# A spectral filter and a gated feed-forward on one core: loads reordered and tables joined at the start of the kernel

## The chip, the cores and the metric

The kernel runs on one core of a Trainium2 chip. The metric is the device time of one execution, in microseconds (us); lower is better. The time before is 865.39 us, the median of 3 runs (865.05 to 866.06).

## The reference

Each of 8 sequences of 3008 rows with 256 channels is filtered in the frequency domain, and every row of the result goes through a normalised, gated feed-forward layer:

```python
X = np.fft.rfft(x, axis=1)                       # x: 8 x 3008 x 256, float32
F = (filt_r + 1j * filt_i)[None, :, :]           # 1505 x 256 each
y = np.fft.irfft(X * F, n=x.shape[1], axis=1)
rows = y.reshape(24064, 256)
xn = rows / sqrt(mean(rows * rows) + 1e-6) * rms_g
g = xn @ w_gate                                  # 256 x 1536
out = (silu(g) * (xn @ w_val)) @ w_out           # 1536 x 256
```

## The kernel before

A transform of length 3008 = 47 x 64 is done in two steps of matrix products, with tables in place of sines. For one sequence b the stages are: the 64-point step of x with the table wa (`a0_unit` for the first sequence, `a_unit` for the others), a turn of the axes, the 47-point step with the middle table wb (`b_unit`), the product with the filter (`s_part`, on the vector engine, DVE, with the filter held transposed in the tile ff), the way back with the tables wi (`bi_unit`) and wai (`n_unit`), and the norm. The feed-forward then runs over items (b, m, jt): 8 sequences, 6 blocks of rows, 12 slices of the 1536 columns. `gv` makes the two first products of an item on the tensor engine (PE), `down` the third.

From the second sequence on, the transform's units are slipped between the items by a planner with costs per engine. The change lies ahead of that: in the part written out by hand for the first sequence, where nothing of the feed-forward can run yet. The whole order is manual; each engine executes its instructions in the order in which they are written.

The loads are issued from two queues, those of SP and of POOL (GpSimd). POOL also computes, and its DMA issues stand in its instruction order; each of its transfers waits until the one issued eight places earlier has landed. In order POOL issues: the four chunks of the first x (`x_load`, L188; float32 in memory, cast to float16, 384 KB each as written), five of six filter calls (`f_load`, L384, 512 KB each: three blocks of rows, imaginary and real part), the middle table wb in two halves (L632), the back table wi (L633), weights (`w_load`, L596), then the filter's negated copies (`f_neg`, L411, and `f_last`, L407), the last weights and the output weights (`wo_load`, L600), the four chunks of the second x (L697), and twelve operations that multiply the weights by the norm's gain (`w_gain`, L608). SP issues the identity idf, the first filter call, the tables wa, ident and wai, and three very short rows, the tails (last row of the filter, gain), all in the first 4 us.

PE works through: five fills (`fill`, a matrix product on zeros whose result is not used, L428), two `f_unit`s (L391: four transposes of a filter block, which ACT, the scalar engine, copies into ff), fills, the six groups of `a0` (L359) with fills and the transposes of the tails (L659, L660) between them, two `f_unit`s, then eight `tr0_unit`s (L369, the turn of the axes; DVE copies each out) alternating with six more `f_unit`s, one more `f_unit`, and then the loop over p. There `b_unit` (L243, tile psb) makes the product with wb, `s_part` on DVE (L233, L236) multiplies by the filter, `yt0_unit` (L420, psy) and `bi_unit` (L287, psi) go on. The list `od` gives the order of the sixteen units; a unit 2g + dh covers four steps of the middle transform, k = 4g to 4g + 3, for the half dh of the channels, and its s_part needs ff for these k and this half: the real part for e = 0, the imaginary part and its negative (from `f_neg`) for e = 1. Every f_unit writes into all k of one half.

After the loop, SP issues four transposing loads (`t4_load`, L301, t<-uu), one for each six rows. The first block of rows takes a way of its own (`t4_first`, `first_norm`), and the second (`n_first`, L485) waits for the first two of these loads and stands on PE behind the third item. From there on PE has items to do without a break.

Of the kernel before, what the change touches and what calls it, by code (L numbers as in the profile page):

```python
# [10 lines left out]
FP32 = mybir.dt.float32  # L11
FP16 = mybir.dt.float16
# [8 lines left out]
P = 128  # L21
# [5 lines left out]
K2 = 32  # L27
# [4 lines left out]
S_INV_A = 0.25  # L32
Y_SCALE = N * S_INV_B * S_INV_A
XC = 6
NXC = H // XC
# [3 lines left out]
def _make_tables():  # L39
    n2 = np.arange(N2)  # L40
    wa = np.zeros((P, P))
    wai = np.zeros((P, P))
    for h in range(2):
        r = slice(h, P, 2)
        for k2 in range(K2):
            c = np.cos(2 * np.pi * ((n2 * k2) % N2) / N2)
            s = np.sin(2 * np.pi * ((n2 * k2) % N2) / N2)
            re = 4 * k2 + 2 * h
            wa[r, re] = c
            wai[re, r] = c * (1.0 if k2 == 0 else 2.0)  # L50
            if k2 == 0:
                alt = 1.0 - 2.0 * (n2 % 2)
                wa[r, re + 1] = alt
                wai[re + 1, r] = alt
            else:
                wa[r, re + 1] = -s
                wai[re + 1, r] = -2.0 * s
    n1 = np.arange(N1)
    rows = (n1 // H) * 2 * H + n1 % H
    re, im = rows, rows + H  # L60
    wb = np.zeros((P, K2, KR))
    wi0 = np.zeros((KR, KR))
    for k2 in range(K2):
        for q in range(SL):
            if q < H:
                k = k2 + 64 * q
                sign = 1.0
            else:
                j = q - H + 1
                k = 64 * j - (k2 if k2 else 32)  # L70
                sign = -1.0
                if j == H and k2:
                    continue
            th = 2 * np.pi * ((n1 * k) % N) / N
            c, sn = np.cos(th), np.sin(th)
            if k == 0 or k == NF - 1:
                sn = np.zeros(N1)
            if k2:
                wb[re, k2, q] = c
                wb[im, k2, q] = sign * sn  # L80
                wb[re, k2, SL + q] = -sn
                wb[im, k2, SL + q] = sign * c
            else:
                part = re if q < H else im
                wb[part, k2, q] = c
                wb[part, k2, SL + q] = -sn
                m = 1.0 if k in (0, NF - 1) else 2.0
                wi0[q, part] = m * c
                wi0[SL + q, part] = -m * sn
    f = np.float16  # L90
    r = np.arange(KR)
    wi = np.zeros((P, K2, KR))
    wi[:KR] = wb[:KR].transpose(2, 1, 0)
    wi[:KR, 0, :] = wi0
    wi[:, :, (r % H) * NR + r // H] = wi * S_INV_B
    return (wa.astype(f), (wai * S_INV_A).astype(f), wb.astype(f), wi.astype(f), np.eye(P).astype(f),
            np.eye(P).astype(np.float32))


@with_exitstack  # L100
def kernel(
# [10 lines left out]
):  # L112
    nc = tc.nc

    wa_np, wai_np, wb_np, wi_np, id_np, if_np = _make_tables()
    wa_d = nc.inline_tensor(wa_np, name="wa_t").ap()
    wai_d = nc.inline_tensor(wai_np, name="wai_t").ap()
    wb_d = nc.inline_tensor(wb_np, name="wb_t").ap()
    wi_d = nc.inline_tensor(wi_np, name="wi_t").ap()
    id_d = nc.inline_tensor(id_np, name="id_t").ap()  # L120
    if_d = nc.inline_tensor(if_np, name="if_t").ap()

    z_d = nc.dram_tensor("z_tmp", (B, K2, KR, D), FP16, kind="Internal").ap()

    glob = ctx.enter_context(tc.tile_pool(name="glob", bufs=1))
# [16 lines left out]
    psM = ctx.enter_context(tc.tile_pool(name="psM", bufs=1, space=bass.MemoryType.PSUM))  # L142
    psB = ctx.enter_context(tc.tile_pool(name="psB", bufs=1, space=bass.MemoryType.PSUM))

    wa = glob.tile([P, P], FP16)
    wai = glob.tile([P, P], FP16)
    ident = glob.tile([P, P], FP16)
    idf = glob.tile([P, P], FP32)
    wb = glob.tile([P, K2, KR], FP16)
    wi = glob.tile([P, K2, KR], FP16)  # L150
    uu = glob.tile([P, H, 2, P], FP16)
# [17 lines left out]
    def raw(src, row, ap):  # L169
        return bass.AP(tensor=src.tensor, offset=src.offset + row * D, ap=ap)  # L170
# [204 lines left out]
    fst = {}  # L375
    FR4 = 4

    def f_load(i, f, eng):
        if i not in fst:
            fst[i] = stg.tile([P, 2, FR4, D], FP32, tag="stg", name="fs")  # L380
        t = fst[i]
        row = FR4 * P * i if i < 2 else NF - 1 - FR4 * P
        for src in ((filt_i, filt_r)[f],):
            eng.dma_start(t[:, f].rearrange("p a d -> p (a d)"),  # L384
                                raw(src, row, [[FR4 * D, P], [1, FR4 * D]]))

    def f_unit(i, f, dh, e):
        t = fst[i]
        ps = bank(1 + "AV".index(e), "psf").rearrange("p (a q) -> p a q", a=FR4)
        for a in range(FR4):  # L390
            nc.tensor.transpose(ps[:, a, :], t[:, f, a, ds(dh * P, P)], idf)  # L391
        v = ps.rearrange("p a (q s) -> p s a q", s=16)
        fk = ff[:, dh, 0:K2].rearrange("p (t k) c -> p t k c", k=4)
        fu = ff[:, dh, 1:K2 + 1].rearrange("p (t k) c -> p t k c", k=4)[:, ::-1, ::-1, :]
        lo = SL * (1 + f) + 8 * i
        hi = lo + H
        if i < 2:
            copy(e, fk[:, :, :, lo:lo + 8], v[:, 0:8])
            copy(e, fu[:, :, :, hi:hi + 8], v[:, 8:16])
        else:  # L400
            copy(e, fk[:, :, :, lo:lo + 8], v[:, 8:16])
            copy(e, fu[:, :, :, hi:hi + 7], v[:, 0:8, :, 1:8])

    def f_last():
        v = ff.rearrange("p e k (s q) -> p e k s q", s=3)
        for dh in range(2):
            nc.gpsimd.tensor_copy(out=v[:, dh, 0, 1:3, H:SL - 1], in_=v[:, dh, K2, 1:3, H:SL - 1])  # L407

    def f_neg(k0, n, dhs=(0, 1)):
        for dh in dhs:  # L410
            nc.gpsimd.tensor_scalar(out=ff[:, dh, k0:k0 + n, 0:SL], in0=ff[:, dh, k0:k0 + n, SL:2 * SL],  # L411
                                    scalar1=-1.0, scalar2=1.0, op0=ALU.mult, op1=ALU.mult)
# [12 lines left out]
    def fill(n, bk=0):  # L425
        ps = bank(bk, "pf")
        for _ in range(n):
            nc.tensor.matmul(ps, ss3[0][:, 0, 0, :], ss3[0].rearrange("p k e q -> p (k e q)")[:, 0:512], start=True, stop=True)  # L428
# [183 lines left out]
    with tc.manual_schedule():  # L612
# [2 lines left out]
        nc.scalar.activation(out=warm, in_=epsb.to_broadcast([P, 4]), func=AXT.Sqrt)  # L615
        for c in range(NXC):
            x_load(0, c)
        nc.sync.dma_start(idf, if_d)
        f_load(0, 0, nc.sync)
        nc.sync.dma_start(wa, wa_d)  # L620
        nc.sync.dma_start(ident, id_d)
        nc.sync.dma_start(wai, wai_d)
        tail = op.tile([P, 4, D], FP32, tag="o3", name="tail")
        for f, src in ((0, filt_i), (1, filt_r)):
            nc.sync.dma_start(tail[0:1, f, :], raw(src, NF - 1, [[D, 1], [1, D]]))
        nc.sync.dma_start(tail[0:2, 2, 0:P], moe_rms_g.rearrange("(a p) -> a p", p=P))
        f_load(0, 1, nc.gpsimd)
        for i in range(1, 3):
            for f in range(2):
                f_load(i, f, nc.gpsimd)  # L630
        for h in range(2):
            nc.gpsimd.dma_start(wb[:, ts(h, K2 // 2), :], wb_d[:, ts(h, K2 // 2), :])  # L632
        nc.gpsimd.dma_start(wi, wi_d)  # L633
        w_load(0)
        w_load(1)
# [10 lines left out]
                for dh in range(2):  # L646
                    a0_unit(gq, dh, E[dh], 1 + dh)

        fill(5)
        for dh in range(2):  # L650
            f_unit(0, 0, dh, "A")
        fill(2)
        a0(0)
        fill(3)
        a0(1, 2)
# [7 lines left out]
        copy("V", gsb, psg[:, 4:6])  # L663
        fill(2)
        a0(3)
        fill(4)
        a0(4, 5)
        for dh in range(2):
            f_unit(0, 1, dh, "A")
        todo = {g: (1, *divmod(g, 2)) for g in range(4)}  # L670
        todo[4], todo[6] = (2, 0, 0), (2, 1, 0)
        for g in range(8):
            tr0_unit(g, "V")
            if g in todo:
                f_unit(*todo[g], "A")
        f_unit(2, 0, 1, "A")
        f_neg(4, 4, (0,))
        f_neg(8, 8, (0,))
        f_neg(4, 4, (1,))
        f_neg(8, 8, (1,))  # L680
        UN = K2 // 2
        od = [2, 4, 3, 5, 6, 7, 0, 1] + list(range(8, UN))
        for p in range(UN + 3):
            if p < UN:
                b_unit(0, od[p], (0, 3)[p % 2])
                s_part(0, od[p], 1)
            if p == 0:
                f_unit(2, 1, 1, "A")
                f_last()
                f_neg(0, 4)  # L690
                w_load(2)
                wo_load(0)
                f_neg(16, 16)
                wo_load(1)
                wo_load(2)
                for c in range(NXC):
                    x_load(1, c)  # L697
                for q in range(3):
                    w_gain(q)
            if p < 2:  # L700
                fill(2, 2)
            if 2 <= p < UN + 1:
                yt0_unit(od[p - 2], "A", 1)
            if p == UN + 1:
                yt0_unit(UN - 1, "V", 1, slice(0, 2))
                yt0_unit(UN - 1, "A", 0, slice(2, 4))
            if 4 <= p < UN + 3:
                bi_unit(0, od[p - 4], "AV"[p == UN + 1], 2)
            if UN + 1 <= p < UN + 3:
                fill(1, 1)  # L710
# [100 lines left out]
        for b in range(1, B):  # L811
            t = (b - 1) * 72
# [73 lines left out]
```

## Time and profile before

| | |
|---|---|
| median of 3 runs | 865.39 us (865.05 to 866.06) |
| the profiled execution's own time | 865.26 us |
| its span, first to last instruction | 863.5 us |
| granted clock of PE, mean | 0.999 |
| busy share of the span: PE, ACT, DVE, POOL | 99%, 71%, 64%, 34% |
| packets on the queues of SP (q1) and POOL (q0) | 190040 and 8352 |

The span runs from the first to the last instruction; some time lies around it. A line of the timeline gives the start in us, the length in us, the engine, the line of the kernel, the operation, the tiles (written <- read), and in brackets how long the engine stood idle before it and what ended that. A line of the transfers gives the tiles, the queue, the operation, the count, the size of one, and the time in us from issue to landing. PE is busy nearly all the time by the page, but fills count as busy, and so do waits inside a group.

In the first 50 us, PE is busy (us, of 5 us each):

```
from     0-10  10-15  15-20  20-25  25-30  30-35  35-40  40-45  45-50
PE       7.21   4.06   5.00   4.94   4.87   5.00   4.67   4.62   4.26
DVE      2.60   3.06   3.36   4.75   5.00   5.00   3.79   2.68   2.14
```

(The first column covers 10 us.) The DMA engines write 198 to 222 GB/s while x is loaded (they read it in float32, twice as many bytes), and 406 to 422 GB/s in the filter calls.

### The profile page before, as it was taken

Reading aid. Unit: us, or ns where it says so; the run is one execution under the profiler, and the core shown is the slowest. Engines: PE = TensorE matmul, PEld = TensorE weight load, DVE = VectorE, ACT = ScalarE, POOL = GpSimd, SP = SyncE. Lnnn points to the kernel's source line nnn. Section 1 sums busy time; section 2 is a strip of 40 time slices with the busy share of each in tenths; the row PEclk is TensorE's granted clock in tenths of the full one; section 3 lists DMA queues with packets and bytes.
Section 4 is the critical chain, followed back from the end, with each engine's and each line's share of the span. In section 5 each row is a group of like instructions: output and inputs, shape, how many; then the busy total and the mean of one; then the engine's idle time right before and its main releaser. Section 6 shows DMA issues by size and latency. Waiting matters only on the chain.

```text
span 863.5 us, 17023 instructions
## 1 busy us (share of the span) xinstructions
PE 852.5 (99%) x6142; PEld 533.2 (62%) x6142; DVE 556.9 (64%) x925; ACT 613.7 (71%) x1340; POOL 296.8 (34%) x344
## 2 busy tenths in 40 slices
PE   8999999999999999999999999999999999999997
PEld 6755666566665666666666666666666666665664
DVE  4857655776666666666666676667666666555554
ACT  5887787777578756887578866888567765777443
POOL 5814841453144321534034430444123430132000
PEclk9999999999999999999999999999999999999999
DMA  9996688775975566646655658433564331521101
GB/s 283 279 179 138 135 168 167 129 137 124 196 146 120 132 150 110 148 110 143 136 127 115 130 103 173 115 87 95 136 127 93 94 72 42 125 53 49 62 25 50
DMA packets 198621, 107.98 MB, mean 125 GB/s; under 512 B 158982, under 2 KB 182920, under 8 KB 198536
## 3 DMA queue, kind: packets, MB, share of 16 engines
q1 hardware_dynamic: 190040, 86.04, 44.4%
q0 software_dynamic: 8352, 20.71, 12.4%
q8 instruction: 48, 0.79, 0.4%
q14 instruction: 37, 0.30, 0.1%
q10 hardware_dynamic: 144, 0.13, 0.0%
HBM read 45.78 MB, written 35.65 MB: 94 GB/s over the span
## 4 chain that ended last, share of the span: by engine, by line
PE 95%; DMA 2%; DVE 1%; ACT 1%; SPq 0%; issue 0%
PE po L565 28%; PE pg L548 28%; PE pv L548 28%; PE psb L243 3%; PE psi L287 2%; PE psn L316 2%; PE psa L208 2%; DMA tail<-in_moe_rms_g_dram 1%; DMA t<-uu 1%; PE psy L420 1%; PE psf L391 0%; PE pst L369 0%; DVE s L233 0%; DVE s L236 0%; DVE hh L553 0%
## 5 line engine op out<-in xcount | busy, mean ns | idle before, releaser
L553 DVE TENSOR_TENSOR hh<-pv,sg 128x512 f16<-128x512 f32 (+2 forms) x578 | 391.7, 678 | 287.3 <-ACT sg L552 222.2
L552 ACT ACTIVATE sg<-pg 128x512 f16<-128x512 f32 (+2 forms) x578 | 337.8, 585 | 216.7 <-PE pg L548 212.4
L548 PE MATMUL pg<-xn,wg 128*128 128x512 f16 (+2 forms) x1156 | 337.9, 374 | 0.0
L548 PE MATMUL pv<-xn,wv 128*128 128x512 f16 (+2 forms) x1156 | 337.8, 374 | 0.0
L565 PE MATMUL po<-wo,hh 128*128 128x256 f16 x2256 | 332.6, 272 | 0.0
L565 PEld LDWEIGHTS <-hh 128*128 128x128 f16 x2256 | 213.5, 98 | 105.3 <-issue 0.6
L270 POOL TENSOR_TENSOR ss<-s,s 128x384 f16<-128x384 f16 x112 | 102.0, 911 | 273.0 <-DVE s L236 245.3
L548 PEld LDWEIGHTS <-wv 128*128 128x128 f16 x1156 | 113.0, 98 | 130.6
L548 PEld LDWEIGHTS <-wg 128*128 128x128 f16 x1156 | 111.5, 98 | 16.9 <-issue 0.2
L342 POOL TENSOR_TENSOR xt<-y,rho 128x1024 f16<-128x1024 f32 (+1 forms) x46 | 85.4, 1857 | 2.9
L324 ACT ACTIVATE junk<-y 128x256 f16<-128x256 f32 x180 | 74.3, 413 | 2.8
L233 DVE TENSOR_TENSOR s<-psb,ff 128x384 f16<-128x384 f32 x124 | 67.8, 547 | 0.0
L236 DVE TENSOR_TENSOR s<-psb,ff 128x384 f16<-128x384 f32 x124 | 67.8, 547 | 0.0
L197 ACT ACTIVATE uu<-psi 128x384 f16<-128x384 f32 (+1 forms) x127 | 61.7, 486 | 1.5 <-PE psb L243 0.5
L197 ACT ACTIVATE y<-psn 128x512 f32<-128x512 f32 (+1 forms) x95 | 55.8, 588 | 4.2
L287 PEld LDWEIGHTS <-yt 96*128 96x128 f16 x512 | 35.4, 97 | 26.7 <-issue 1.0
L334 POOL TENSOR_TENSOR rho<-u,mhalf 128x4 f32<-128x4 f32 (+1 forms) x46 | 46.5, 1010 | 3.8
L332 POOL TENSOR_SCALAR u<-ss 128x4 f32<-128x4 f32 (+1 forms) x46 | 8.9, 194 | 104.3 <-ACT junk L324 103.3
L197 ACT ACTIVATE t<-psa 128x512 f16<-128x512 f32 x71 | 42.0, 595 | 3.2 <-PE psa L208 1.7
L287 PE MATMUL psi<-wi,yt 96*128 96x96 f16 x512 | 42.9, 205 | 0.1
L243 PE MATMUL psb<-wb,t 96*128 96x96 f16 x480 | 40.2, 206 | 0.5 <-DVE s L236 0.3
L243 PEld LDWEIGHTS <-t 96*128 96x128 f16 x480 | 28.7, 97 | 13.8 <-DVE s L236 3.9
(98 smaller groups left out, 366.1 us busy)
## 6 DMA issues: line engine op xcount, KB each, us to landing
out_dram<-o SPq DMA_DIRECT2D x40, 512.0 KB, 3.6
xc<-in_x_dram POOLq DMA_DIRECT2D x31, 384.0 KB, 6.0
z_tmp<-t SPq DMA_DIRECT2D x28, 384.0 KB, 2.6
t<-z_tmp SPq DMA_DIRECT2D x28, 384.0 KB, 6.1
out_dram<-o SPq DMA_DIRECT2D x7, 384.0 KB, 2.7
fs<-in_filt_r_dram POOLq DMA_DIRECT2D x3, 512.0 KB, 12.1
ws<-in_moe_w_gate_dram POOLq DMA_DIRECT2D x3, 512.0 KB, 11.5
ws<-in_moe_w_val_dram POOLq DMA_DIRECT2D x3, 512.0 KB, 11.7
```

The source lines that it names most:

```text
L197: nc.scalar.activation(out=out, in_=in_, func=AXT.Copy, **({} if scale is None else {"scale": scale}))
L233: eng.tensor_tensor(out=o, in0=ps, in1=f1, op=ALU.mult)
L236: eng.tensor_tensor(out=o, in0=ps[:, :, ::-1, :], in1=f2, op=ALU.mult)
L243: nc.tensor.matmul(ps[:, ts(k, KR)], st[b]["t2"][kk // KC][:, kk % KC, ds(dh * P, P)], wb[0:KR, kk, :], start=True, stop=True)
L270: nc.gpsimd.tensor_tensor(out=ss3[g % 3][:, :, dh, 0:KR], in0=s[0], in1=s[1], op=ALU.add)
L287: nc.tensor.matmul(ps[:, k, :], yt[0:KR, k, dh, :], wi[0:KR, 4 * g + k, :], start=True, stop=True)
L324: nc.scalar.activation(out=junk, in_=y[:, i, ts(u, D)], func=AXT.Square, accum_out=ss[:, 2 * i + u:2 * i + u + 1])
L342: nc.gpsimd.tensor_tensor(out=xt[:, 0:n, :], in0=y.rearrange("p a (u d) -> p (a u) d", u=2)[:, 0:n, :], in1=rho[:, 0:n].unsqueeze(2).to_br ...
L548: nc.tensor.matmul(ps[:, 0:w], wt[:, dt_, ts(jt, P)], xn[:, q0:q1, dt_, :], start=(dt_ == 0), stop=(dt_ == 1))
L552: nc.scalar.activation(out=sg[:, c], in_=pg[:, 0:w], func=AXT.Silu)
L553: nc.vector.tensor_tensor(out=hh[:, c], in0=pv[:, 0:w], in1=sg[:, c], op=ALU.mult)
L565: nc.tensor.matmul(po[s4 // 2][:, s4 % 2, :], hh[:, ts(s4, P)], wo[:, jt, :], start=(jt == 0 and s4 % 2 == 0), stop=(jt == JT - 1 and (s4 ...
```

## The change

- Four small arrays become one: wa, wai, ident and the float32 identity are one array of 128 x 640 float16 (`tab`), loaded by one DMA on SP; the tiles are views of it. Ahead of the tails, SP now issues one load where it issued five.
- All six filter calls are issued by POOL, behind the first x.
- The middle table is loaded as 8 and 24 of its 32 steps in place of two halves of 16, and the 8 go ahead of the sixth filter call.
- On PE the two f_units that stood ahead of the first a0 go behind the last; ten fills in place of five and two stand at the start, and three in place of four ahead of the last a0. The eight f_units of the first two blocks and one of the third alternate with the tr0_units; one more of the third precedes the loop over p, and two follow the first b_unit.
- `od` begins 2, 3, 4 in place of 2, 4, 3; the negated copies are made in another order, three of the four early ones behind the first b_unit.
- On POOL the third and fourth chunk of the second x are issued behind the twelve gain operations.

```diff
+    tab = np.concatenate([wa.astype(f), (wai * S_INV_A).astype(f), np.eye(P).astype(f),
+                          np.eye(P).astype(np.float32).view(f)], axis=1)
+    return tab, wb.astype(f), wi.astype(f)
...
+    tab = glob.tile([P, 5 * P], FP16)
+    wa, wai, ident = (tab[:, ts(i, P)] for i in range(3))
+    idf = tab[:, 3 * P:5 * P].bitcast(FP32)
...
-        nc.sync.dma_start(idf, if_d)
-        f_load(0, 0, nc.sync)
-        nc.sync.dma_start(wa, wa_d)
-        nc.sync.dma_start(ident, id_d)
-        nc.sync.dma_start(wai, wai_d)
+        nc.sync.dma_start(tab, tab_d)
...
-        f_load(0, 1, nc.gpsimd)
-        for i in range(1, 3):
-            for f in range(2):
-                f_load(i, f, nc.gpsimd)
-        for h in range(2):
-            nc.gpsimd.dma_start(wb[:, ts(h, K2 // 2), :], wb_d[:, ts(h, K2 // 2), :])
+        for n in range(6):
+            if n == 5:
+                nc.gpsimd.dma_start(wb[:, 0:8, :], wb_d[:, 0:8, :])
+            f_load(*divmod(n, 2))
+        nc.gpsimd.dma_start(wb[:, 8:K2, :], wb_d[:, 8:K2, :])
...
-        fill(5)
-        for dh in range(2):
-            f_unit(0, 0, dh, "A")
-        fill(2)
+        fill(10)
         a0(0)
...
-        fill(4)
+        fill(3)
         a0(4, 5)
-        for dh in range(2):
-            f_unit(0, 1, dh, "A")
-        todo = {g: (1, *divmod(g, 2)) for g in range(4)}
-        todo[4], todo[6] = (2, 0, 0), (2, 1, 0)
+        todo = [(i, f, dh) for i in range(2) for f in range(2) for dh in range(2)]
+        for u in todo[0:2]:
+            f_unit(*u, "A")
+        todo = {g: u for g, u in enumerate(todo[2:] + [(2, 0, 0)])}
         for g in range(8):
             tr0_unit(g, "V")
             if g in todo:
                 f_unit(*todo[g], "A")
-        f_unit(2, 0, 1, "A")
+        f_unit(2, 1, 0, "A")
         f_neg(4, 4, (0,))
-        f_neg(8, 8, (0,))
-        f_neg(4, 4, (1,))
-        f_neg(8, 8, (1,))
         UN = K2 // 2
-        od = [2, 4, 3, 5, 6, 7, 0, 1] + list(range(8, UN))
+        od = [2, 3, 4, 5, 6, 7, 0, 1] + list(range(8, UN))
...
             if p == 0:
+                f_unit(2, 0, 1, "A")
                 f_unit(2, 1, 1, "A")
+                f_neg(4, 4, (1,))
+                f_neg(8, 8)
...
-                for c in range(NXC):
+                for c in range(2):
                     x_load(1, c)
                 for q in range(3):
                     w_gain(q)
+                for c in range(2, 4):
+                    x_load(1, c)
```

More of the change, by code (lines that the diff above doesn't have):

```diff
@@ L95, in _make_tables @@
     wi[:, :, (r % H) * NR + r // H] = wi * S_INV_B
-    return (wa.astype(f), (wai * S_INV_A).astype(f), wb.astype(f), wi.astype(f), np.eye(P).astype(f),
-            np.eye(P).astype(np.float32))
+    tab = np.concatenate([wa.astype(f), (wai * S_INV_A).astype(f), np.eye(P).astype(f),
+                          np.eye(P).astype(np.float32).view(f)], axis=1)
+    return tab, wb.astype(f), wi.astype(f)
 @with_exitstack
@@ L113 @@
     nc = tc.nc
-    wa_np, wai_np, wb_np, wi_np, id_np, if_np = _make_tables()
-    wa_d = nc.inline_tensor(wa_np, name="wa_t").ap()
-    wai_d = nc.inline_tensor(wai_np, name="wai_t").ap()
+    tab_np, wb_np, wi_np = _make_tables()
+    tab_d = nc.inline_tensor(tab_np, name="tab_t").ap()
     wb_d = nc.inline_tensor(wb_np, name="wb_t").ap()
     wi_d = nc.inline_tensor(wi_np, name="wi_t").ap()
-    id_d = nc.inline_tensor(id_np, name="id_t").ap()
-    if_d = nc.inline_tensor(if_np, name="if_t").ap()
     z_d = nc.dram_tensor("z_tmp", (B, K2, KR, D), FP16, kind="Internal").ap()
@@ L143 @@
     psB = ctx.enter_context(tc.tile_pool(name="psB", bufs=1, space=bass.MemoryType.PSUM))
[L145 to L148, printed above, removed]
+    tab = glob.tile([P, 5 * P], FP16)
+    wa, wai, ident = (tab[:, ts(i, P)] for i in range(3))
+    idf = tab[:, 3 * P:5 * P].bitcast(FP32)
     wb = glob.tile([P, K2, KR], FP16)
@@ L376, with f_load @@
     FR4 = 4
-    def f_load(i, f, eng):
+    def f_load(i, f):
         if i not in fst:
@@ L383, in f_load @@
         for src in ((filt_i, filt_r)[f],):
-            eng.dma_start(t[:, f].rearrange("p a d -> p (a d)"),
+            nc.gpsimd.dma_start(t[:, f].rearrange("p a d -> p (a d)"),
                                 raw(src, row, [[FR4 * D, P], [1, FR4 * D]]))
```

## The prediction

> **What bounds the kernel now.** I read the page first (PE busy 99% of the span of 863.5 us, 95% of the chain that ended last), then that chain in order of time, then the timeline and the landing of single transfers in the first 60 us, the only stretch in which the changed lines run. Of the chain (start, length, what):
>
> ```profile
> 3.75 7.59 DMA tail<-in_moe_rms_g_dram
> ...
> 14.43 1.07 PE psf L391 x8
> ...
> 21.84 0.62 DVE t2o L199
> 22.51 0.56 DVE s L233
> ...
> 42.16 6.04 DMA t<-uu
> 48.24 0.40 PE psn L485 x4
> ```
>
> The reader sees three limits in turn: arrivals up to 14.4 us, PE and DVE up to 42, then a transposing transfer of L301 that holds PE at 48.24. From there PE is full. What the change is worth is therefore read from one number: when the second L485 group can start. The timeline has PE's part of it:
>
> ```profile
> 13.28 1.06 PE L359 MATMUL psa<-wa,xc 128*128 128x128 f16 x16
> 14.43 1.07 PE L391 MATMUL psf<-idf,fs 128*128 128x128 f32 x8
> ...
> 47.11 0.40 PE L485 MATMUL psn<-wai,t 128*128 128x128 f16 x4
> 48.24 0.40 PE L485 MATMUL psn<-wai,t 128*128 128x128 f16 x4 [0.74 <-DMA t<-uu]
> ```
>
> The first L485 group starts where the work before it ends; the second finds PE idle for 0.74 us. So an earlier start can win 0.74 us and whatever the first 47 us shrink by, but only if that transfer also lands earlier; each us that it lands later is lost one for one.
>
> **The start of the kernel.** The x loads (L188) are issued by POOL from 1.25 us. The fourth is issued at 3.11 and lands 9.9 us later, at 13.0; the third lands near 11.1, so one x load takes 1.9 us of the DMA engines. SP's first filter call comes in ahead of x. What x would do alone, an x load issued at 53.38 with nothing ahead of it shows (first line; 53.38 to 58.1); one issued at 226.40 took 5.4 (second line):
>
> ```profile
> xc<-in_x_dram POOLq DMA_DIRECT2D x1, 384.0 KB, 4.7
> ...
> xc<-in_x_dram POOLq DMA_DIRECT2D x1, 384.0 KB, 5.4
> ```
>
> Nothing in the trace shows an x load first in an empty queue, so I bound it by these two and take 4.7, as only one small table load precedes it: x lands at 5.95, 7.85, 9.75 and 11.65 (upper bound 12.35), against 13.0. The filter calls behind it took 1.3 us each before (landing at 14.3, 15.55, 16.85, 18.1, 19.4): now 12.95, 14.25, 15.55, 16.8, 18.1, then 0.5 for a quarter of the middle table (two halves of 384 KB took near 1.0 each), and the sixth call at 19.9, 0.5 later than the last one before.
>
> The single table array costs nothing: SP has four issues of 0.36 to 0.45 us fewer ahead of the tail loads, which landed at up to 11.38 and held PE for 0.85 us. That wait goes, but its gain is inside the x gain, since the next a0 group needs the third x anyway. Two more fills (18 for 16, 0.21 to 0.43 each) run while PE waits for x; without that cover they would cost 0.4 to 0.9.
>
> **The filter calls on PE.** Before, the first filter group after a0 starts at 14.43, 1.4 after the last x landed. Now 11.65 + 1.4 = 13.05, and its data are there at 12.95. But more work now lies behind it. Between 14.43 and the first psb at 22.08 stood 8 tr0 units and 9 f_units at 0.445 each (17 x 0.445 = 7.6); now 8 and 10: the first psb at 13.05 + 18 x 0.445 + 0.1 = 21.15, a gain of 0.93. The second b_unit is now the odd half of the group (od begins 2, 3 instead of 2, 4), so it needs the very last f_unit: that one starts near 21.9, ends 22.5, and ACT needs 0.66 for each of the last two, to 23.4. DVE then starts the second unit at 23.45, against 23.51. After it DVE runs without a gap in both (0.93 per unit). So of the 1.4 us that x arrives earlier, next to nothing (0.06) reaches the loop of b_units: 0.9 goes to two f_units that used to fill the wait for x, the rest to ACT's pair.
>
> One row makes it worse. Instructions come in by DMA too (48 packets on q8 in the page, one for each 250 or so of PE's instructions). The packet records show the first, of 16 KB at 19.39 that took 1.08 us, and from then on one DMA engine ends about 1.6 us behind the others: the middle table's first half landed 2.55 after the last filter call, for 0.95 of data. The same place in PE's program comes near 18.6 now, and then it is the sixth filter call that is late: 21.5 for 19.9, with PE ready for it at 20.7. That would put the b_units 0.75 later than before. I give it six in ten; the bounds of this part are thus -0.6 (x landing as early as the data allow) and +0.8.
>
> **The second x and POOL.** POOL before:
>
> ```profile
> 30.13 2.47 POOL L188 DMA_DIRECT2D xc<-in_x_dram  x4
> 32.36 1.64 POOL L608 TENSOR_SCALAR wg<-ws,gsb 128x512 f16<-128x512 f32 x2
> ...
> 40.35 0.41 POOL L296 COPY left<-uu 128x128 f16<-128x128 f16 x1
> ```
>
> Two x issues (0.62 each) move from 31.4 to behind the twelve gain operations, which then end 1.25 earlier. Ahead of them f_neg now waits once for ACT and has 0.42 more to do in that place: +0.3, or +1.05 with the late filter call. So the two x loads are issued near 39.4 (40.15) and 40.0 (40.8). Behind them on POOL stand only the copy of L296 and the rho of L505, 11.6 us later: no price there. Their users, the a_units of the third and fourth chunk, run after 55: none either.
>
> The price is on the DMA engines. SP issues the transposing loads at 39.57. Before, x queued until 44.1 (its last chunk, issued at 31.97, took 12.1), the first chunk of t landed at 47.06 and the second at 48.2. Now the last x ends, by the 4.7 row, at 39.4 + 4.7 + 1.9 = 46.0 or, with the late filter call, at 46.75; by the 5.4 row at 47.45 at most: 1.9 to 3.35 later than before. I take 46.4, between the first two. Whether a transposing load waits for x that was issued about the same time, another place shows. Behind the x load of 226.40, a store and a transposing load landed like this, and without x (issued at 223.09) like the third line:
>
> ```profile
> out_dram<-o SPq DMA_DIRECT2D x1, 512.0 KB, 6.3
> t<-uu SPq DMA_TRANSPOSE x1, 7.1
> ...
> t<-uu SPq DMA_TRANSPOSE x1, 4.9
> ```
>
> The packet records agree: from 227.5 to 230.7 x packets alone. So SP's transfers stand behind x. Before, the second chunk landed 4.1 after x ended; 1.1 of that was a stop from 45.5 to 46.7 at an instruction packet. Without the stop: 46.4 + 3.0 = 49.4, which is 1.2 later than 48.2. With it 50.5 and more; if the transposing load comes first (-2), 47.3.
>
> [...]
>
> **Sum.** b_units 0 to +0.75, hidden under the wait at 48; wait of L485 for t: +1.2. 863.5 + 1.2 = 864.7 of span; the same execution took 865.26 and the median of three is 865.39, 0.13 away. Prediction 866.5.
>
> **The rivals.**
> - *Slower beyond doubt*: the late filter call and the instruction packet both hit. The x loads go out at 40.15, end at 47, and the stop of 1.1 still follows: chunk two at 47 + 4.1 = 51.1, +2.9, 868.2. For it: both packets come at a place of PE's program, not at a time. Against: the second one may pass while t waits anyway. It decides once x ends after 46.8.
> - *No change*: the transposing loads are paced by SP's issue (2.5 to 3.2 us each before) and by that stop, not by x. Then 48.2 stays: 865.3. Against: single loads of this kind took 4.4 to 4.9, not 7.5.
> - *Faster*: t's first chunk enters before x (39.57 against 39.4 to 40.15 is close) and passes. PE then never waits: -0.74, and with x landing early another -0.6 to -1.1: 864.5 to 863.5, middle 864.1.
> - *That part of it does nothing*: if the first x still starts only at 4.0, as its packets did before, x lands about 0.6 later than I say; the sum at 48 stays.
>
> **Chances.** Forecast (865.8 to 867.2 is its own range) 0.40; slower rival 0.22; no change 0.14; faster rival 0.24. About 0.2% or 1.7 us is what a measurement here tells from no change. Slower by more: the slower rival and a third of the forecast, 0.35. Faster by more: half of the faster rival, 0.13. Within: 0.52. Range 864.0 to 868.3, which leaves out the ends of both outer rivals.
>
> **What would show it.** Right: first L359 near 6, last x landing near 11.7, the f_unit after a0 near 13.05, first psb between 21.1 and 22, DVE's second unit no earlier than 23.4, the second L485 near 49.4 with over 1.5 us idle before it. Wrong: if the second L485 starts before 48, the collision did not happen; if psb starts before 20.5, I have overrated the f_units; if the time differs by what nothing before 50 us shows, the whole reading fails.

## The result and the profile after

The changed kernel takes 870.40 us (median of 6 runs, 869.30 to 871.53) beside 865.22 us (median of 6, 864.76 to 866.06) of the kernel before: ratio 1.006, 95% interval 1.0047 to 1.0073. It is slower by about 5.2 us. The profiled execution took 870.39 us, its span is 868.6 us, 5.1 more than before, and the mean granted clock of PE is 0.998.

Line numbers from here on are those of the changed kernel where it is read: the 47-point product psb is L240 (L243 before), s_part L230 and L233 (L233, L236), a filter unit L388 (L391), the back product psn of the norm block L482 (L485), the transposing load L298 (L301). The chain of work that ended last, in order of time (start, length, what), shows where the limits lie now:

```profile
2.59 7.05 DMA xc<-in_x_dram
9.93 11.20 DMA fs<-in_filt_r_dram
...
23.98 0.56 DVE s L230
...
41.80 10.40 DMA t<-uu
52.25 0.61 PE psn L482 x4
```

New are the x load at its head, where a tail load stood, and the last filter call, up to 21.1; the transposing transfer takes 10.40 where it took 6.04. The units between them stand as they did. The timeline of PE has the same from the engine's side (start, length, operation, idle time before it and what ended that):

```profile
5.96 0.62 PE L356 MATMUL psa<-tab,xc 128*128 128x128 f16 x8 [0.81 <-DMA xc<-in_x_dram]
...
11.54 0.96 PE L356 MATMUL psa<-tab,xc 128*128 128x128 f16 x14 [0.47 <-DMA xc<-in_x_dram]
12.93 1.06 PE L388 MATMUL psf<-tab,fs 128*128 128x128 f32 x8 [0.43 <-DMA fs<-in_filt_i_dram]
...
21.27 0.63 PE L388 MATMUL psf<-tab,fs 128*128 128x128 f32 x4 [0.53 <-DMA fs<-in_filt_r_dram]
21.73 0.34 PE L240 MATMUL psb<-wb,t 96*128 96x96 f16 x4
...
47.07 0.59 PE L545 MATMUL pv<-xn,wv 128*128 128x512 f16 x2
50.88 0.40 PE L482 MATMUL psn<-tab,t 128*128 128x128 f16 x4 [3.22 <-DMA t<-uu]
52.25 0.61 PE L482 MATMUL psn<-tab,t 128*128 128x128 f16 x4 [0.97 <-DMA t<-uu]
52.65 1.06 PE L562 MATMUL po<-wo,hh 128*128 128x256 f16 x4
```

Up to 13 us the start is 1.5 us ahead of before (the first filter group after a0 stood at 14.43), at the first psb 0.35 ahead (21.73 for 22.08), and DVE's second unit is 0.47 late (23.98 for 23.51). PE's last ready product ends at 47.66 (50.88 less 3.22), 0.55 later than the first psn group started before; then PE waits 3.22 and 0.97 us, where it waited 0.74. The last line tells of a second loss: four products of 128x256 take 1.06 us there; the same group took 0.60 before, as its line there shows:

```profile
48.48 0.60 PE L565 MATMUL po<-wo,hh 128*128 128x256 f16 x4
```

The table by stretches says why (stretch, us, then busy time of PE, PEld, DVE, ACT and POOL, and last the granted clock, the DMA share and GB/s):

```profile
48.00:50.00 2.00, 0.00 (x0) 0.00 (x0) 0.65 (x1) 0.00 (x0) 0.00 (x0) 1.00 1.13 89
...
52.00:54.00 2.00, 1.75 (x10) 1.24 (x11) 0.00 (x0) 1.10 (x3) 0.00 (x0) 0.51 1.12 215
54.00:56.00 2.00, 2.00 (x10) 0.96 (x9) 0.47 (x1) 1.07 (x2) 0.00 (x0) 0.64 0.51 94
```

From 48 to 50 PE does nothing, and the DMA engines are busy but move 89 GB/s. From 52 on the granted clock is half (0.50 from 52.1 to 55.4): 0.51 and 0.64 as means of two stretches of 2 us make 1.96 and 1.44 us at half clock, 3.4 us in all. Behind 60 us no wait of PE differs from before. The transfers that were in flight at that time (tiles, queue, operation, size, us from issue to landing):

```profile
xc<-in_x_dram POOLq DMA_DIRECT2D x1, 384.0 KB, 5.2
xc<-in_x_dram POOLq DMA_DIRECT2D x1, 384.0 KB, 9.7
...
t<-uu SPq DMA_TRANSPOSE x1, 10.8
t<-uu SPq DMA_TRANSPOSE x1, 10.4
```

The two moved x loads landed at 45.23 and 50.24, the two chunks of t at 50.84 and 52.20 (47.06 and 48.20 before). So the second chunk is 4.0 us late, and PE's second psn group with it (52.25 for 48.24). The two transposing loads were issued about when they were before (at 40.05 and 41.80, for 39.57 and 42.16), so it is their transfer that is late, not their start. Behind the second psn group PE loses 1.55 us more, at the lower clock: its last group of products starts 5.56 us later than before (timeline of the changed kernel, then of the kernel before).

```profile
862.43 1.47 PE L562 MATMUL po<-wo,hh 128*128 128x256 f16 x12
```

```profile
856.87 1.47 PE L565 MATMUL po<-wo,hh 128*128 128x256 f16 x12
```

The span grows by 5.1 and not by 5.56, because in the profiled execution of the kernel before the time from the end of that group to the end of the span is 0.4 us longer.

### The profile page after: what moved, and what is told of

The parts are those of the page before. It is cut to its first block, busy times and chain, and to the rows that moved or that the text cites. A ratio compares the mean times of both kernels' runs of the same rounds, so it can differ in the third digit from the quotient of the medians.

```text
span 868.6 us, 17024 instructions
## 1 busy us (share of the span) xinstructions
PE 854.0 (98%) x6144; PEld 532.8 (61%) x6144; DVE 557.0 (64%) x925; ACT 613.8 (71%) x1340; POOL 297.5 (34%) x345
## 4 chain that ended last, share of the span: by engine, by line
PE 94%; DMA 3%; DVE 1%; ACT 1%; issue 0%; POOL 0%; SPq 0%; POOLq 0%
PE po L562 28%; PE pg L545 28%; PE pv L545 28%; PE psb L240 3%; PE psi L284 2%; PE psn L313 2%; PE psa L205 2%; DMA fs<-in_filt_r_dram 1%; DMA t<-uu 1%; DMA xc<-in_x_dram 1%; PE psy L417 1%; DVE s L233 0%; DVE hh L550 0%; DVE s L230 0%; ACT sg L549 0%
## 5 line engine op out<-in xcount | busy, mean ns | idle before, releaser
L230 DVE TENSOR_TENSOR s<-psb,ff 128x384 f16<-128x384 f32 x124 | 67.8, 547 | 1.5 <-ACT ff L194 1.5
L233 DVE TENSOR_TENSOR s<-psb,ff 128x384 f16<-128x384 f32 x124 | 67.8, 547 | 0.0
L331 POOL TENSOR_TENSOR rho<-u,mhalf 128x4 f32<-128x4 f32 (+1 forms) x46 | 46.5, 1011 | 3.8
L240 PE MATMUL psb<-wb,t 96*128 96x96 f16 x480 | 40.2, 206 | 0.5 <-DVE s L233 0.3
L240 PEld LDWEIGHTS <-t 96*128 96x128 f16 x480 | 28.7, 97 | 13.9 <-DVE s L233 3.8
```

Of the source, the lines that this page charges most:

```text
L230: eng.tensor_tensor(out=o, in0=ps, in1=f1, op=ALU.mult)
L233: eng.tensor_tensor(out=o, in0=ps[:, :, ::-1, :], in1=f2, op=ALU.mult)
L240: nc.tensor.matmul(ps[:, ts(k, KR)], st[b]["t2"][kk // KC][:, kk % KC, ds(dh * P, P)], wb[0:KR, kk, :], start=True, stop=True)
```

## The experiments

The theory after this reading: (1) the two x loads behind the gain operations meet the transposing loads on the DMA engines, and each holds the other up; (2) PE's long wait then lowers its clock; (3) the new order at the start gives next to nothing. Rivals: the new start itself is slower; the single table array or the new order of units costs time; the x loads are an innocent bystander of an instruction packet of 16 KB. In each block of experiments the kernel before was run again on the same chip: 865.50 us (median of 21) in the first, 865.67 us (median of 33) in the second, 865.55 us (one run) in the third.

**All x loads back ahead of the gain operations, the rest of the change kept (e1_x_back).**

```diff
-                for c in range(2):
+                for c in range(NXC):
                     x_load(1, c)
                 for q in range(3):
                     w_gain(q)
-                for c in range(2, 4):
-                    x_load(1, c)
```

> The changed kernel with all four chunks of the second x issued ahead of the gain operations again; the new start stays. Theory (the two late x loads hold the transposing loads of t): the second chunk of t lands between 47.5 and 49.5, as before the change, the second L482 group starts there, PE's clock stays at 1.0, and the time is 865.0 to 866.3. Rival (the new start with its late sixth filter call costs the time): 869 or more, with t landing late all the same.

Measured 865.61 us (865.01 to 865.90, 11 runs), ratio 1.0001 (0.9992 to 1.001). The last x landed at 44.40, the chunks of t at 47.38 and 48.54. The timeline of PE has the wait of before again, and quick products behind it (0.60, as before, at a granted clock of 1.00):

```profile
48.58 0.40 PE L482 MATMUL psn<-tab,t 128*128 128x128 f16 x4 [0.76 <-DMA t<-uu]
48.82 0.60 PE L562 MATMUL po<-wo,hh 128*128 128x256 f16 x4
```

So the whole loss hangs on the place of these two loads, and all other parts of the change together are worth nothing in time, within 0.1%, as long as PE waits for t.

**Only this part, in the kernel before (e2_x_alone).**

```diff
-                for c in range(NXC):
+                for c in range(2):
                     x_load(1, c)
                 for q in range(3):
                     w_gain(q)
+                for c in range(2, 4):
+                    x_load(1, c)
```

> The kernel before with nothing but the third and fourth chunk of the second x moved behind the gain operations. Theory (x behind the gain operations holds t): t's second chunk lands at 50.5 to 52.5, PE waits 3 to 5 us at L485, 868.5 to 871. Rival (only both parts together are slow, because the new start is 0.5 late): below 867.

Measured 871.47 us (870.05 to 873.01, 4 runs), ratio 1.0069 (1.0055 to 1.0083): the part alone does all of the damage, a little more than in the changed kernel and than was expected (up to 871). The profiled execution is the slowest of the four, with a longer wait of PE than in the changed kernel and the low clock behind it for twice as long: the granted clock is 0.87, 0.50, 0.50, 0.50 and 0.93 in the stretches of 2 us from 50 to 60, which makes 6.8 us at half clock (timeline, L485 in this file):

```profile
52.46 0.61 PE L485 MATMUL psn<-wai,t 128*128 128x128 f16 x4 [4.36 <-DMA t<-uu]
53.82 0.61 PE L485 MATMUL psn<-wai,t 128*128 128x128 f16 x4 [0.75 <-DMA t<-uu]
54.23 1.06 PE L565 MATMUL po<-wo,hh 128*128 128x256 f16 x4
```

**The changed kernel with sixteen fills in PE's wait (e3_warm).** They do not shorten the wait; they only keep PE busy in it.

```diff
+        at(2, fill, 16)
         at(2, n_first, 1)
```

> The changed kernel with 16 more fills on PE ahead of the first group that waits for t (about 3.5 us of unused products in a stretch in which PE stands idle for 3.2). Nothing arrives earlier. Theory (the granted clock falls to 0.5 after the idle stretch and PE runs at half speed from 52.3 to 55.4, which costs 1.1 to 1.3 of the 5.1): clock 1.0 throughout, 869.0 to 869.5. Rival (all of the loss is the wait): 870.2 or more.

Measured 868.56 us (868.23 to 868.88, 4 runs), ratio 1.0035 (1.0021 to 1.0049): 1.84 us less than the changed kernel, more than expected. The timeline:

```profile
47.44 3.62 PE L425 MATMUL pf<-ss 128*128 128x512 f16 x16
51.12 0.38 PE L482 MATMUL psn<-tab,t 128*128 128x128 f16 x4
52.10 0.40 PE L482 MATMUL psn<-tab,t 128*128 128x128 f16 x4 [0.60 <-DMA t<-uu]
52.33 0.60 PE L562 MATMUL po<-wo,hh 128*128 128x256 f16 x4
```

The second psn group starts 0.15 earlier than without the fills (52.10 for 52.25), and the products behind it are quick again (0.60 for 1.06); the granted clock is 1.00 from 48 to 54. Between the two spans lie 1.6 us (868.6 to 867.0; 3.4 us at half clock would lose 1.7). Of the 5.6 us by which PE's last products are late in the changed kernel, some 1.6 thus belong to the clock and 4.0 to the wait itself.

**As e1, with two fills in place of ten at the start (e4_few_fills).** It asks whether the first 16 KB instruction packet, at 18.47, comes at a count of PE's instructions.

```diff
-        fill(10)
+        fill(2)
         a0(0)
```

> As e1_x_back, with two fills in place of ten at the start (eight products less ahead of everything, 16 PE instructions). Theory (a 16 KB instruction packet comes at a place of PE's program and makes one DMA engine late, and the sixth filter call with it): the packet comes near 19.3 in place of 18.5, the sixth call lands at 19.8 to 20.3 in place of 21.1, and the first psb starts up to 0.9 earlier; the time is the same as e1 or up to 0.8 less. Rival (the engine is late at a time of its own, or the call is late for another reason): it lands at 21.1 again.

Measured 865.35 us (865.09 to 866.04, 11 runs), ratio 1.0000 (0.9991 to 1.0009). The packet came at 18.45 with some 26 of PE's recorded instructions fewer ahead of it, and the sixth filter call landed at 21.09 as before. The idea of a count fell; what sets the packet's time is open. That a late DMA engine and this packet belong together stays an association: no run moved the one without the other. For the time it does not matter, since e4 and e1 agree.

**The fourth x load after the wait, the other three ahead of the gain operations (e5_x3_far), and the same one move in the kernel before (e6_before_x3_far).** If the collision is the cause, one load fewer in the queue at 40 us must also end the 0.74 us that PE waited before the change.

```diff
-                for c in range(2):
+                for c in range(3):
                     x_load(1, c)
                 for q in range(3):
                     w_gain(q)
-                for c in range(2, 4):
-                    x_load(1, c)
...
         at(4, q_unit, 1)
+        at(5, x_load, 1, 3)
```

> The changed kernel with three chunks of the second x ahead of the gain operations and the fourth behind the rho of the second block, where POOL comes at about 53, after both chunks of t have landed. Theory (an x load holds t only while it is in the queue together with t, and t's wait is now all that an earlier start could win back): x ends near 40.6, t's second chunk lands by 47, no wait at L482, 864.3 to 865.0. Rival (what holds t is something else, SP's own issue or the instruction packet near 45): second chunk at 48 or later, 865.3 or more.

> The kernel before with the same move of the fourth chunk, so that no wait for t hides the b_units: against e5_x3_far it shows what the new start is worth by itself. Theory (the earlier x is eaten up by two more f_units ahead of the b_units, the late sixth call and ACT's last two copies): DVE's second unit starts at 23.5 here and at 23.9 to 24.0 there, and this kernel is 0.2 to 0.6 faster than e5. Rival (the new start wins what x wins, 1 us or more): this kernel is 0.5 or more slower than e5.

Measured 864.24 us (864.12 to 864.47, 11 runs; ratio 0.9982, 0.9973 to 0.9991) with the changed start, and 864.60 us (863.96 to 865.18, 11 runs; ratio 0.9985, 0.9976 to 0.9994) with the old one. In both the two psn groups run as one, with no idle time in front (timeline of e5, then of e6):

```profile
24.05 0.56 DVE L230 TENSOR_TENSOR s<-psb,ff 128x384 f16<-128x384 f32 x1 [0.36 <-ACT ff L194]
...
47.57 0.61 PE L482 MATMUL psn<-tab,t 128*128 128x128 f16 x8
```

```profile
24.10 0.56 DVE L233 TENSOR_TENSOR s<-psb,ff 128x384 f16<-128x384 f32 x1
...
47.62 0.61 PE L485 MATMUL psn<-wai,t 128*128 128x128 f16 x8
```

The second chunk of t landed at 47.43 and 47.24. In e5 the last x ahead of the gain operations landed at 43.25 and not, as expected, near 40.6, so x and t (issued at 40.11) still lay in the queues together for some 3 us: the overlap is shorter there, not gone. I had expected the old start to be the faster by 0.2 to 0.6 us; it is 0.36 slower by the medians, with ranges that overlap. The profiled execution of e6 began 0.6 later than that of the kernel before (24.10 for 23.51), which is within what its executions differ by (1.2 us; those of e5 lie within 0.35). So the new start is worth between nothing and 0.4 us once the wait is gone, and its eleven times lie closer together.

**e5 with the old order of the units (e7_od_back).** The prediction said that the second unit, now the odd half of the group, has to wait for the very last filter unit. Here `od` begins 2, 4, 3 again, and the negated copies and fills go with it.

```diff
         f_neg(4, 4, (0,))
+        f_neg(8, 8, (0,))
-        od = [2, 3, 4, 5, 6, 7, 0, 1] + list(range(8, UN))
+        od = [2, 4, 3, 5, 6, 7, 0, 1] + list(range(8, UN))
...
-                f_neg(8, 8)
+                f_neg(8, 8, (1,))
...
-            if p < 2:
+            if p == 1:
                 fill(2, 2)
```

> As e5_x3_far, with the order of the units of before (od begins 2, 4, 3), its f_neg for it, and no fills behind the first unit. Theory (DVE's gap of 0.4 between first and second unit is the price of the new order): the second unit starts at 23.5 to 23.6, the whole is 0.3 to 0.5 faster than e5. Rival (PE or ACT holds the second unit just as long): same as e5.

Measured 863.88 us (863.69 to 864.00, 11 runs), ratio 0.9979 (0.9970 to 0.9988): 0.36 less than e5, with ranges that do not touch, and the fastest version of all, ahead of the kernel before by 1.8 us. DVE's second unit follows the first without the gap of 0.36 us, and PE reaches the psn groups 0.6 earlier. The fills behind the first unit are gone here too, and the run does not separate them from the order (timeline):

```profile
23.46 0.55 DVE L230 TENSOR_TENSOR s<-psb,ff 128x384 f16<-128x384 f32 x1
...
46.97 0.61 PE L482 MATMUL psn<-tab,t 128*128 128x128 f16 x8
```

**Only the fourth x load behind the gain operations (e8_one_late).**

```diff
-                for c in range(2):
+                for c in range(3):
                     x_load(1, c)
                 for q in range(3):
                     w_gain(q)
-                for c in range(2, 4):
+                for c in range(3, 4):
                     x_load(1, c)
```

> The changed kernel with only the fourth chunk of the second x behind the gain operations, half of the dose. Theory (t waits for the end of x, wherever that is): the fourth chunk lands at 45.3 to 46.5 alone behind the gain operations, t's second chunk at 48.5 to 50.5, 865.5 to 868. Rival (any x load issued next to t costs the same): 869 or more.

Measured 867.92 us, median of 10 runs that lie between 865.77 and 870.66 (ratio 1.0024, 1.0009 to 1.0039): four lie at 865.8 to 866.2, two between, four at 869.5 to 870.7. The median is within what was expected, but it stands for no execution. The profiled one took 869.52; its x load landed at 50.36 and not, as expected, by 46.5 (timeline):

```profile
50.42 0.40 PE L482 MATMUL psn<-tab,t 128*128 128x128 f16 x4 [2.88 <-DMA t<-uu]
51.63 0.61 PE L482 MATMUL psn<-tab,t 128*128 128x128 f16 x4 [0.81 <-DMA t<-uu]
```

So a single load issued at 40.4 can cost nearly as much as two, or next to nothing. Three more executions of this kernel were profiled to see what decides (e9_look_a, e9_look_b, e9_look_c).

> The kernel of the experiment with one late x load once more, to get a profile of a quick execution (its times lay in two groups, near 866 and near 870). Theory A, the order on the DMA engines decides: in an execution near 866 the late x load has its packets behind it before the transposing loads have theirs (x landed by 46, second chunk of t by 48.7, wait of PE under 1 us), and the 16 KB instruction packet may come at any time. Theory B, the instruction packet decides: in an execution near 866 it falls outside 44 to 50 us or on an engine that has no x left, and in one near 870 it falls inside. If both kinds of execution show x trickling out in the same way, neither holds.

> As for the first look: 865.7 to 870.7 us; near 866 the second chunk of t lands by 48.7, near 870 between 51 and 52.5; A reads it from when the late x load lands, B from where the 16 KB packet falls.

> As for the first look: 865.7 to 870.7 us; near 866 the second chunk of t lands by 48.7, near 870 between 51 and 52.5; A reads it from when the late x load lands, B from where the 16 KB packet falls.

They took 869.40, 868.91 and 868.54 us. None was quick, so what tells a quick execution from a slow one is not settled. What the four profiled executions have in common is an order: the late x load landed at 50.36, 50.15, 49.44 and 49.04, and the second chunk of t 1.2, 1.3, 1.1 and 1.1 us later. In all four a 16 KB instruction packet comes in PE's wait or up to 0.6 us ahead of it (at 48.30, 48.28, 47.37 and 46.94), so order (theory A) and packet (theory B) are not told apart. A landing is not the end of x's packets either: in e9_look_a, b and c the last x packet starts at 48.04, 47.14 and 46.99, over 2 us ahead of the landing, and in between t stands nearly still without any x, just behind the instruction packet (30 packets of t from 49.0 to 50.0 in e9_look_a, 68 from 47.0 to 48.5 in e9_look_c). The same stop stands in a run that loses nothing: in e1, 25 packets of t from 46.0 to 47.0, behind the instruction packet at 45.16. So the packet alone does not make the loss; whether it makes more of it where x is late is open.

The packet records of the first of the three show how x holds t, well ahead of the instruction packet of that execution (start in us, queue q0 of POOL or q1 of SP, bytes, ns; a selection in order):

```
44.636  q1   256   31
44.663  q0  3072  247
44.823  q1   256  269
44.829  q1   256  269
44.834  q1   256  275
44.891  q1   256   31
44.918  q0  3072  247
45.088  q1   256  251
45.094  q1   256  511
45.147  q1   256   31
45.174  q0  3072  247
```

The x packets (3072 bytes) come strictly one behind the other, each followed by one quick packet of t: that is one DMA engine on which x and t take turns, one packet each, 0.255 us a round. Every other packet of t in this stretch lasts about one round or two (241 to 276 ns, or 492 to 512), and they end together, just ahead of the next quick one. Undisturbed, such a packet takes 18 ns (the median from 40 to 49 us in the kernel before). The engine writes 8 of the 128 packets of the load, from 44.15 to 46.19, ahead of all others. So while a single engine writes x, the transposing load moves on all engines at the pace of that one: 29 to 34 packets of t in half a microsecond between 44.5 and 46.0, against 566 in e1 at 44.5, when x was done. The records don't name the engine; that it is one, and that the others wait for it, is read from the order of starts and ends.

In the changed kernel the same balance is seen with x on all engines: from 45.5 to 47.0, 79 packets of t against 79 of x. But turns are not the whole of it. From 41.35 to 43.2 the changed kernel has 60 packets of x and none of t, though t was issued at 40.05; e9_look_c has 69 of x and none of t from 44.5 to 45.5; and in e9_look_a the other engines write x from 46.5 to 48.0 with 94 packets against 47 of t. There t stands behind x. What decides between the two is open; either way t is late while x is under way.

The execution of e9_look_c also shows a low clock behind a shorter wait. First its timeline, then the table by stretches, with the granted clock as the third number from the end:

```profile
49.08 0.40 PE L482 MATMUL psn<-tab,t 128*128 128x128 f16 x4 [1.54 <-DMA t<-uu]
50.15 0.40 PE L482 MATMUL psn<-tab,t 128*128 128x128 f16 x4 [0.67 <-DMA t<-uu]
50.38 0.60 PE L562 MATMUL po<-wo,hh 128*128 128x256 f16 x4
50.82 0.99 PE L545 MATMUL pg<-xn,wg 128*128 128x512 f16 x2
```

```profile
50.00:52.00 2.00, 1.85 (x11) 1.02 (x12) 0.00 (x0) 1.58 (x4) 0.00 (x0) 0.72 1.24 263
52.00:54.00 2.00, 2.00 (x8) 1.03 (x7) 0.69 (x1) 0.65 (x2) 0.00 (x0) 0.50 0.19 36
54.00:56.00 2.00, 2.00 (x19) 1.18 (x18) 0.83 (x2) 1.19 (x2) 0.06 (x1) 0.93 0.00 0
```

Here idle times of 1.54 and 0.67 us stand ahead of the whole price: 1.12, 2.0 and 0.28 us at half clock by the three rows, 3.4 us again, from about 50.9 on. In e1 one idle time of 0.76 us brought nothing of the kind (1.00 in every stretch from 44 to 60).

## Why the prediction was right and wrong

**What bounds the kernel: right.** The change was to be read from one number, the start of the second psn group; it moved by 4.0 us, the span by 5.1, and nothing behind 60 us differs.

**x first: right.** Landing at 5.92, 7.77, 9.64 and 11.50, for 5.95, 7.85, 9.75 and 11.65. The price of 4.7 us, borrowed from an x load at 53 us, was good to 0.15 in this execution; in the other runs with the new start the fourth x landed at 11.54 to 12.04.

**Filter calls and units: right.** The first five calls landed within 0.2 of the forecast (12.79 to 17.93). The sixth, with six chances in ten of being late, was late: its last part landed at 21.13, one engine behind the others, next to a 16 KB instruction packet at 18.47. First psb 21.73 (21.15 to 22), DVE's second unit 23.98 (23.45, or 24.2 with the late call). That the odd half waits for the last filter unit is seen in the line of e5 (0.36 us, ended by ACT's copy into ff) and gone in e7, which brings DVE's second unit forward by 0.6, of which 0.14 lies ahead of the first unit already, and the time by 0.36 us. The reason given for the packet (a place in PE's program) fell with e4, so that its time came out (18.47 for 18.6) is luck as far as the runs show.

**The table array and the added fills cost nothing: supported**, as e1 and e4 agree with the kernel before, though the array was not undone alone, and PE's wait for t would hide a small cost in both.

**POOL: right.** The late x loads were issued from 40.02 on (39.4, or 40.15 with the late call). The last x of the kernel before was issued at 31.79 and took 12.3, not at 31.97 and 12.1 as the prediction has it; the landing at 44.1, on which the sum rests, is right.

**x ends at 46.4: wrong, and this is the step that failed.** The first of the two landed at 45.23, 0.7 later than the step has it (46.4 less 1.9). The second landed 5.0 behind it instead of 1.9. The step priced the two loads from places where no transfer of SP's moved beside x (no packet of its queue from 11.5 to 13.0, nor from 54.2 to 57.4, in the kernel before); here the transposing loads were issued at the same time (40.05) and shared the engines with x (79 packets of each from 45.5 to 47.0). How much of the 5.0 belongs to the instruction packet at 46.52, behind which the last 20 packets of x took from 47.5 to 49.6, is open. The next step, t = x end + 3.0, was too long for its part: t landed 1.96 behind x. Together: 0.7 + 3.1 - 1.0 = 2.8, which is the difference between 49.4 and 52.20. The term "wait of L485 for t: +1.2" measured +4.0.

**How x and t share the engines: half right.** From the rows at 227.5 the prediction had SP's transfers stand behind x. In some stretches t did (60 packets of x and none of t from 41.35 to 43.2 in the changed kernel). In others the two took turns: by the packet records of e9_look_a from 44.2 to 46.2, on an engine with both, 247 ns of x and 31 ns of t alternate. Taking turns did not make t early there: a turn of t moved 256 bytes and one of x 3072, and by the same records t on the other engines waited for that turn too. Neither picture has what was missing in the sum, that x itself took longer beside t: the second load landed 5.0 us behind the first, where 1.9 was priced.

**The clock: not foreseen.** The prediction had a wait of some 2 us in it (0.74 + 1.2) and did not ask what follows. The wait of 4.2 us cost a further 1.6 (e3), so "each us that it lands later is lost one for one" did not hold: 4.0 us became 5.6 at PE's last products. The granted clock fell to 0.50 for 3.4 us in the changed kernel (idle times of 3.22 and 0.97 us) and in e9_look_c (1.54 and 0.67), and for twice that in e2 (4.36 and 0.75); with 0.74 in the kernel before and 0.76 in e1 it stayed at 1.00. How much idle time it takes, between 0.76 us and the 2.2 of e9_look_c in two pieces with work between, was not shown. Even the wait that was forecast is thus near one that lowered the clock.

**The rivals.** "Slower beyond doubt" had the mechanism nearest to the truth: late x loads and an instruction packet (46.52) on top, with +2.9 and 868.2. What it lacks is the second x load's 9.7 us (+1.1 more on t) and the clock. "No change" is refuted by e1 and e2: the time follows the place of the x loads. "Faster" is refuted, as PE waited longer; in e9_look_a t's first packets did go ahead of most of the late x load (t moved from 44.5 on, and 94 of the load's 128 packets came from 46.5 to 48.0), and yet t was late, because a chunk started is not a chunk landed. "That part does nothing" is refuted by the first a0 group at 5.96. Forecast and result have the same sign; 866.5 became 870.4 through a term of +1.2 that is +4.0, and a term for the clock that was missing.

## What to carry to other kernels

A bulk load that has many microseconds of slack should not be issued next to a transposing load on which the tensor engine will wait: one load moved behind that wait won 1.1 us (e6, 865.67 to 864.60), two moved to just before it lost 6.0 (e2, 865.50 to 871.47). When two transfers of different queues overlap, do not price each as if it were alone (the second late x load landed 5.0 us behind the first, where 1.9 was priced), and ask what the slowest engine does to the rest (e9_look_a: 29 to 34 packets of t in half a microsecond while one engine wrote x, against 566 in e1). And when a wait of the tensor engine grows to a few microseconds, add a slow clock behind it (3.4 us at 0.50 with 2.2 us idle in e9_look_c and 4.2 in the changed kernel, 6.8 with 5.1 in e2), or fill the wait (e3: 1.8 us for a line).

## What was not expected of the hardware

- By the order of its packets, the transposing load moved in step on the DMA engines: while one engine wrote x, the packets of t took 241 to 512 ns in place of 18, but for the quick ones between the x packets (e9_look_a, 44.5 to 46.0).
- The same program lands in times 5 us apart when such loads start within a microsecond of each other: e8 has 865.77 and 870.66. With the load out of the way the spread is 0.35 us or less with the new start (e5, e7), and 1.22 with the old one (e6).
- The first 16 KB instruction packet comes near 18.4 us in all kernels with the new start (18.33 to 18.72), with some 26 recorded instructions fewer ahead of it too (e4), and lasts 1.0 to 1.1 us on one engine. What sets its time is open.
